# Hedgehog linear attention with a gated feed-forward: the order of work in the load stage, and 28 and 6 unused matmuls in place of 24 and 14

## The chip, the cores and the metric

The kernel runs on one core of one Trainium2 chip. Its time is the device time of one execution in microseconds (us). Before the change three timed runs gave 1631.84 us (median), 1631.5 and 1634.65 us. A further execution, taken by the hardware profiler, took 1630.73 us, of which 1628.6 us lie between its first and its last instruction (its span). All stages below are told in us from the start of that span.

## The reference

Float32 throughout; x has 2048 rows of 576.

```python
def _A_ref(x, wqkv, w_phi, wo):           # linear attention, 32 heads of 18
    q, k, v = split(x @ wqkv)
    pq, pk = q @ w_phi, k @ w_phi         # per head
    phi_q = concat([softmax(pq), softmax(-pq)])
    phi_k = concat([softmax(pk), softmax(-pk)])
    num = phi_q @ (phi_k.T @ v)
    den = phi_q @ sum(phi_k) + 1e-6
    return (num / den) @ wo
def _B_ref(x, w_gate, w_up, w_down):      # 4608 hidden columns
    return (silu(x @ w_gate) * (x @ w_up)) @ w_down
xn = layernorm(x)
return x + _A_ref(xn, ...) * silu(_B_ref(xn, ...))
```

## The kernel before, in words

The program has four stages: load, K and V, Q, and the feed-forward. Only the load stage, the first 69 us, is touched. It brings x and the attention weights into SBUF, normalises x, and turns everything into pairs of a rounded main part (fp32r, "hi", written by a ScalarE cast) and a remainder ("lo", what the cast lost, written by a subtraction on VectorE or GpSimd). Every product of the kernel is then hi·hi + lo·hi + hi·lo.

**x** comes in four blocks of 512 rows, in the order 2, 3, 0, 1; a block is four tiles `xn` of 128 rows. `norm_stats` (lines 173 to 186) makes the statistics on VectorE: two `bn_stats` for each tile, one `bn_aggr`, then six small steps (lines 180 to 186) that end with 1/sqrt in `rs` and the shift in `rt`; the square root in the middle (line 181) is on ScalarE and needs its own activation table. `norm_block` (lines 188 to 219) normalises the four tiles, two on VectorE (line 194) and two on ScalarE (line 191); GpSimd copies the last columns of each tile (line 197); TensorE transposes the tiles into three PSUM buffers `tp`, 24 transposes in all (line 206); ScalarE casts the main parts into `X` (lines 208, 213) and copies the last third to `xr` (line 214); VectorE writes the remainders of the first two thirds (line 209) and GpSimd those of the last (line 216). The function returns the last transpose (`last`), the second remainder on VectorE (`rest`) and the `xr` copy (`copy`).

**The K weights, and later the Q weights,** are multiplied by the feature map at once: `fold` (lines 228 to 238) does five groups of six matmuls of w_qk with the block-diagonal `PHI`, each group into one `tp` buffer, and takes each out with a cast on ScalarE and two subtractions on VectorE (`split_rows`, lines 62 to 65). There are three `tp` buffers for all transposes and folds, so a group starts when the subtractions of the group three before it are through.

**The V weights** come in six pieces `wst` (five buffers, shared with the w_qk pieces). Each is cast on ScalarE into `KVWH` (line 266); four of the remainders are on GpSimd (line 268), two on VectorE (line 270).

**Early tiles.** Two of the 36 hidden column tiles of the feed-forward are computed for blocks 2 and 3 in this stage (lines 116 to 128), which gives TensorE something to do between folds and transposes: for each column tile and each block 14 matmuls for the gate half and 14 for the up half (line 93), a Silu on ScalarE (line 122, another activation table) and a multiplication on VectorE (line 126). Their weights are `raw`, split into `wh` and `wl` by `early_weights` (lines 101 to 114). They use the two PSUM buffers `pe`.

**Unused matmuls** (`keep_clock`, line 141) multiply zeros: 24 at the program's start and 14 behind block 2's transposes. Nothing reads their result.

The order of the instructions on each engine is made by a scheduler from the order in which the code is written, with two means to bend it: `tc.high_priority()` prefers what stands inside it, and `tc.issue_after(i)` puts what stands inside it behind instruction `i`. On the chip each engine takes its own queue strictly in order, and so does the SP engine, which issues the loads.

Of the kernel before, what the change touches and what calls it, by code (L numbers as in the profile page):

```python
# [12 lines left out]
AF = mybir.ActivationFunctionType  # L13
ALU = mybir.AluOpType
# [20 lines left out]
LN_EPS = 1e-5  # L35
# [12 lines left out]
def gated_hedgehog_kernel(ctx: ExitStack, tc, x, w_qk, w_v, w_phi, wo, w_gu, w_tail, w_down, ident_in, mask_in, out):  # L48
# [66 lines left out]

    def early_tile(f, i, parts, js=(0, 1), banks=None, store=nc.sync, behind=None):
        for j in js:
            pg, pu = banks or [eps.tile([P, BT], F32, name="pe") for _ in range(2)]
            xw(pg, i, j, slice(0, BT), *parts[0], False)
            h = epool.tile([P, BT], F32, name="h")  # L120
            with tc.high_priority():
                nc.scalar.activation(h, pg, AF.Silu)
            last = xw(pu, i, j, slice(0, BT), *parts[1], False)
            with tc.issue_after(behind.ins) if behind else ExitStack():
                with tc.high_priority():
                    nc.vector.tensor_mul(h, pu, h)
            store.dma_start(h_dram[i, f, :, j * BT:(j + 1) * BT], h)
        return last

    outs = []  # L130
    with ExitStack() as att:
# [17 lines left out]
        with ExitStack() as wst:  # L149
# [4 lines left out]
            with ExitStack() as pst:  # L154
# [10 lines left out]
                def load_x(b):  # L165
# [5 lines left out]
                    return xns  # L171

                def norm_stats(bs, xns):
                    t = slice(4 * bs[0], 4 * bs[-1] + 4)
# [4 lines left out]
                    var, r, q = mv[:, t, 1], rs[:, t], rt[:, t]  # L179
                    nc.vector.tensor_scalar_add(var, var, LN_EPS)  # L180
                    nc.scalar.activation(r, var, AF.Sqrt)
                    nc.vector.reciprocal(r, r)
                    nc.vector.tensor_mul(q, r, r)
                    nc.vector.scalar_tensor_tensor(q, q, -0.5, var, op0=ALU.mult, op1=ALU.mult)
                    nc.vector.scalar_tensor_tensor(r, q, 1.5, r, op0=ALU.add, op1=ALU.mult)
                    return nc.vector.scalar_tensor_tensor(q, mv[:, t, 0], -1.0, r, op0=ALU.mult, op1=ALU.mult)

                def norm_block(b, xns):
                    for n, (i, xn) in enumerate(zip(range(4 * b, 4 * b + 4), xns)):
                        if n % 2:  # L190
                            nc.scalar.activation(xn[:, 0:D], xn[:, 0:D], AF.Identity, bias=rt[:, i:i + 1],
                                                 scale=rs[:, i:i + 1])
                        else:
                            nc.vector.tensor_scalar(xn[:, 0:D], xn[:, 0:D], mv[:, i, 0:1], rs[:, i:i + 1],
                                                    op0=ALU.subtract, op1=ALU.mult)
# [43 lines left out]

                keep_clock(24)  # L240
                xns = load_x(2)
# [21 lines left out]
                for n in range(6):  # L263
                    k, c = divmod(n, 3)
                    src, vh = wv[n][:, 0:D], KVWH[:, k, c, D:2 * D]
                    nc.scalar.copy(vh, src)
                    if c < 2:
# [8 lines left out]
                for f in range(2):  # L276
                    early_tile(f, 1, first_weights[f], store=nc.gpsimd)

# [850 lines left out]
```

## Time and profile before

| what | value |
|---|---|
| timed runs, median (lowest to highest) | 1631.84 us (1631.5 to 1634.65) |
| profiled execution: own time, span | 1630.73 us, 1628.6 us |
| granted TensorE clock, mean | 0.999 |
| busy over the span: TensorE, VectorE, ScalarE, GpSimd | 99%, 72%, 44%, 40% |
| the chain that ended last | TensorE 94%, VectorE 3%, DMA 1%, ScalarE 1% |
| first matmul of the K and V stage starts at | 69.29 us |

TensorE's share is an average over the program. It is not full in the first 40 us, and the change lies wholly there; so the question is when the load stage lets TensorE go, not what TensorE does later. In a timeline row the columns are start, duration, engine, line and operation, tiles written from tiles read, the count of instructions merged into the row, and in brackets the idle time of the engine before it and what ended it. A row that merges several instructions shows their summed extent.

### The profile page before, as it was taken

How to read it: one execution, taken by the hardware profiler on the slowest of the kernel's cores; microseconds unless marked ns; L12 is line 12 of the kernel's file. 1: busy time of each engine (PE TensorE's matmuls, PEld its weight loads, DVE VectorE, ACT ScalarE, POOL GpSimd, SP SyncE). 2: the span in 40 equal slices, each digit the busy share in tenths (PEclk: the TensorE clock that was granted, in tenths of full speed). 3: DMA queues.
4: the chain of work that ended last, by engine and by line, in shares of the span. 5: the costliest groups of instructions: out<-in, count | busy, mean ns of one | idle time of the engine just before them, and what ended most of it. 6: DMA issues, size and time to landing. Idle time of an engine off the chain costs nothing.

```text
span 1628.6 us, 25267 instructions
## 1 busy us (share of the span) xinstructions
PE 1609.0 (99%) x9422; PEld 1430.2 (88%) x9423; DVE 1172.9 (72%) x1721; ACT 722.1 (44%) x1391; POOL 655.5 (40%) x704
## 2 busy tenths in 40 slices
PE   8999999999999999999999999999999999999998
PEld 5999998999987888888888888888888888888887
DVE  7677769899854678878777778825666766666578
ACT  5633345544433654444454444455433333333334
POOL 4566652434123446446445355313233314133132
PEclk9999999999999999999999999999999999999999
DMA  9522243434247645555454454685454655555444
GB/s 304 190 80 79 93 144 108 127 105 125 62 154 286 214 155 173 171 186 178 167 187 171 161 193 150 249 268 154 140 169 124 203 180 179 168 182 179 141 116 174
DMA packets 121484, 268.46 MB, mean 165 GB/s; under 512 B 12786, under 2 KB 53362, under 8 KB 119570
## 3 DMA queue, kind: packets, MB, share of 16 engines
q1 hardware_dynamic: 106076, 245.44, 45.9%
q0 software_dynamic: 3392, 12.07, 2.6%
q10 hardware_dynamic: 11894, 9.35, 1.8%
q8 instruction: 74, 1.21, 0.3%
q14 instruction: 48, 0.39, 0.1%
HBM read 167.19 MB, written 99.61 MB: 164 GB/s over the span
## 4 chain that ended last, share of the span: by engine, by line
PE 94%; DVE 3%; DMA 1%; ACT 1%; issue 0%; POOL 0%; SPq 0%; ACTq 0%; POOLq 0%; DVEq 0%
PE px L730 24%; PE pd L855 24%; PE pw L730 12%; PE p L93 7%; PE pe L93 7%; PE py L730 6%; PE p L633 4%; PE kvp L312 2%; PE po L613 2%; PE vx L400 1%; PE pt L607 1%; PE vw L400 1%; PE tp L235 1%; PE vy L93 1%; PE vx L93 1%
## 5 line engine op out<-in xcount | busy, mean ns | idle before, releaser
L855 PEld LDWEIGHTS pd<-dw,hh 128*128 128x128 f32 x3048 | 432.5, 188 | 24.2 <-ACT pd L876 1.5
L855 PE MATMUL pd<-dw,hh 128*128 128x288 f32 x3048 | 448.3, 297 | 2.3 <-ACT pd L876 0.7
L730 PE MATMUL px<-X,w 128*128 128x512 f32 x1488 | 384.4, 393 | 2.5 <-ACT s L759 1.4
L730 PEld LDWEIGHTS px<-X,w 128*128 128x128 f32 x1488 | 270.5, 188 | 54.9 <-ACT s L759 3.8
L730 PE MATMUL pw<-X,w 128*128 128x512 f32 x732 | 188.7, 393 | 0.0
L730 PEld LDWEIGHTS pw<-X,w 128*128 128x128 f32 x732 | 137.0, 189 | 30.5
L764 DVE TENSOR_TENSOR s<-pw,s 128x512 f32<-128x512 f32 x124 | 85.1, 688 | 99.6 <-ACT s L759 88.8
L980 DVE TENSOR_TENSOR acc<-pd,acc 128x576 f32<-128x576 f32 x128 | 96.3, 753 | 82.9 <-PE pd L855 82.8
L759 ACT COPY s<-px 128x512 f32<-128x512 f32 x124 | 72.6, 585 | 157.9 <-PE px L730 157.8
L60 DVE TENSOR_TENSOR hh<-ha,hh 128x512 fp32r<-128x512 f32 x140 | 110.9, 818 | 20.7 <-ACT hh L59 19.1
L59 ACT CAST hh<-ha 128x512 fp32r<-128x512 f32 x140 | 82.6, 619 | 92.3 <-PE pd L855 73.6
L93 PE MATMUL pe<-X,wh 128*128 128x512 f32 (+1 forms) x380 | 119.6, 398 | 2.2 <-DVE X L209 1.0
L952 POOL TENSOR_TENSOR hb<-hb 128x512 f32<-128x512 f32 x34 | 46.5, 1368 | 165.7 <-DVE hb L776 161.3
L60 DVE TENSOR_TENSOR w<-ld,w 128x512 fp32r<-128x512 f32 (+1 forms) x93 | 77.2, 831 | 35.8 <-ACT w L59 34.7
L730 PE MATMUL px<-X,wt 96*128 96x512 f32 x248 | 97.9, 395 | 0.0
L730 PE MATMUL py<-X,w 128*128 128x512 f32 x372 | 96.4, 393 | 0.0
L965 POOL TENSOR_TENSOR ha<-ha 128x512 f32<-128x512 f32 x34 | 52.6, 1562 | 106.2 <-DVE hh L60 106.2
L939 POOL TENSOR_TENSOR h<-ha,hb 128x512 f32<-128x512 f32 x34 | 44.3, 1303 | 123.9 <-DVE ha L780 88.6
L59 ACT CAST w<-ld 128x512 fp32r<-128x512 f32 (+1 forms) x93 | 51.0, 549 | 89.6 <-POOL ld L720 58.0
L93 PEld LDWEIGHTS pe<-X,wh 128*128 128x128 f32 (+1 forms) x380 | 69.8, 189 | 16.1 <-DVE X L209 1.4
L784 ACT COPY py<-px 128x512 f32<-128x512 f32 x62 | 35.5, 572 | 102.6 <-PE px L730 85.0
L717 POOL TENSOR_TENSOR ts<-ld 128x256 f32<-128x256 f32 x31 | 28.7, 926 | 125.7 <-issue 68.5
(267 smaller groups left out, 3251.9 us busy)
## 6 DMA issues: line engine op xcount, KB each, us to landing
w_dram<-w SPq DMA_DIRECT2D x90, 512.0 KB
w<-w_dram SPq DMA_DIRECT2D x90, 512.0 KB
wt<-t_dram SPq DMA_DIRECT2D x61, 336.0 KB
ld<-in_B_w_gu SPq DMA_DIRECT2D x31, 512.0 KB
X<-sum_dram SPq DMA_DIRECT2D x8, 1280.0 KB
rt<-in_B_w_down SPq DMA_DIRECT2D x33, 288.0 KB
rb<-in_B_w_down SPq DMA_DIRECT2D x33, 288.0 KB
w_dram<-w SPq DMA_DIRECT2D x30, 256.0 KB
```

Of the source, the lines that this page charges most:

```text
L59: nc.scalar.copy(hi, src)
L60: nc.vector.tensor_sub(lo, src, hi)
L93: last = nc.tensor.matmul(ps, l, r, start=n == 0, stop=n == len(pairs) - 1)
L633: nc.tensor.matmul(ps[:, 0:HALF], a[0:w, g, jc], bw[0:w, g, n], start=k == 0, stop=k == 3 * NG - 1)
L730: nc.tensor.matmul(ps, l, r, start=first and n == 0, stop=last and n == len(mm) - 1, skip_group_check=True)
L759: nc.scalar.copy(t, ps)
L764: nc.vector.tensor_add(t, ps, t)
L855: nc.tensor.matmul(ps, l, r, start=first and n == 0 and m == 0, stop=n == len(hs) - 1 and m == 2, skip_group_check=True)
L939: sub(s, g["h"][0][0], g["h"][0][1])
L952: nc.gpsimd.tensor_add(a21, a21, g["h"][1][1])
L965: sub(a12, a12, g["h"][0][0])
L980: nc.vector.tensor_add(a2, pd[:, :, 0:HALF], a2)
```

## The change

Five edits, all in the load stage:

1. The first run of unused matmuls has 28 instead of 24, the second 6 instead of 14.
2. The statistics of block 3 are put behind the second VectorE remainder of block 2 (`rest`), where they stood behind the last small step of block 2's statistics; the small steps are at high priority.
3. The second early column tile's weights (`early_weights(1)`) are put behind block 3's `xr` copy.
4. The six casts of the V weights are put behind the same copy.
5. The Silu of the first early column tile for each block is held behind the second ScalarE normalisation of block 3.

```diff
-    def early_tile(f, i, parts, js=(0, 1), banks=None, store=nc.sync, behind=None):
+    def early_tile(f, i, parts, js=(0, 1), banks=None, store=nc.sync, hold=None, behind=None):
...
-            with tc.high_priority():
-                nc.scalar.activation(h, pg, AF.Silu)
+            with tc.issue_after(hold.ins) if hold else ExitStack():
+                with tc.high_priority():
+                    nc.scalar.activation(h, pg, AF.Silu)
...
+                    with tc.high_priority():
+                        nc.vector.tensor_scalar_add(var, var, LN_EPS)
+                        roots.append(nc.scalar.activation(r, var, AF.Sqrt))
...
-                keep_clock(24)
+                keep_clock(28)
...
-                chain = norm_stats([2], xns[0:4])
+                norm_stats([2], xns[0:4])
                 last, rest, _ = norm_block(2, xns[0:4])
                 with tc.issue_after(last.ins):
-                    keep_clock(14)
+                    keep_clock(6)
+                with tc.issue_after(rest.ins):
+                    norm_stats([3], xns[4:8])
                 first_weights = [early_weights(0)]
-                with tc.issue_after(chain.ins):
-                    norm_stats([3], xns[4:8])
                 fold(wk, KVWH[:, :, :, 0:D], KVWL[:, :, :, 0:D])
-                norm_block(3, xns[4:8])
-                first_weights.append(early_weights(1))
+                _, _, copy = norm_block(3, xns[4:8])
+                first_weights.append(early_weights(1, copy))
...
-                    nc.scalar.copy(vh, src)
+                    with tc.issue_after(copy.ins):
+                        nc.scalar.copy(vh, src)
...
-                    early_tile(f, 1, first_weights[f], store=nc.gpsimd)
+                    early_tile(f, 1, first_weights[f], store=nc.gpsimd, hold=None if f else norms[3])
```

What this makes of the queues is seen at three places. Line numbers of the changed kernel are one to five higher than those of before from line 122 on.

VectorE, at block 2's remainders (X_64 and X_65 are its two X buffers). Before:

```order
L194 TENSOR_SCALAR xn<-xn,mv,rs 128x576 x2
L177 BN_STATS stats<-xn 128x6
L209 TENSOR_TENSOR X_64<-tp,X_64 128x1024
L209 TENSOR_TENSOR X_65<-tp,X_65 128x1024
L177 BN_STATS stats<-xn 128x6 x2
```

Now:

```order
L198 TENSOR_SCALAR xn<-xn,mv,rs 128x576 x2
L213 TENSOR_TENSOR X_64<-tp,X_64 128x1024
L213 TENSOR_TENSOR X_65<-tp,X_65 128x1024
L180 BN_STATS stats<-xn 128x6 x3
L181 BN_AGGR mv<-stats 128x2
```

One `bn_stats` of block 3 has moved from ahead of the two remainders to behind them.

VectorE, from the second step before the end of block 3's statistics to block 3's normalisation, while the K fold is taken out (KVWL, KVWH). Before:

```order
L185 SCALAR_TENSOR_TENSOR rs<-rt,rs 128x4
L177 BN_STATS stats<-xn 128x6
L186 SCALAR_TENSOR_TENSOR rt<-mv,rs 128x4
L64 TENSOR_TENSOR KVWL<-tp,KVWH 128x4x126
L64 TENSOR_TENSOR wl<-raw,wh 128x512
L65 TENSOR_TENSOR wh<-raw,wh 32x2x128
L65 TENSOR_TENSOR KVWH<-tp,KVWH 32x2x126
L64 TENSOR_TENSOR KVWL<-tp,KVWH 128x4x72
L65 TENSOR_TENSOR KVWH<-tp,KVWH 32x2x72
L194 TENSOR_SCALAR xn<-xn,mv,rs 128x576 x2
```

Now:

```order
L189 SCALAR_TENSOR_TENSOR rs<-rt,rs 128x4
L65 TENSOR_TENSOR KVWH<-tp,KVWH 32x2x126
L190 SCALAR_TENSOR_TENSOR rt<-mv,rs 128x4
L64 TENSOR_TENSOR KVWL<-tp,KVWH 128x4x126
L65 TENSOR_TENSOR KVWH<-tp,KVWH 32x2x126
L64 TENSOR_TENSOR KVWL<-tp,KVWH 128x4x72
L65 TENSOR_TENSOR KVWH<-tp,KVWH 32x2x72
L198 TENSOR_SCALAR xn<-xn,mv,rs 128x576 x2
```

A `bn_stats` of block 0 and the two subtractions of the second early weights (wl, wh) are gone from ahead of the normalisation; they stand behind it now.

ScalarE, from block 3's square root to its X casts. Before:

```order
L266 CAST KVWH<-wst 128x576
L181 ACTIVATE rs<-mv 128x4
L266 CAST KVWH<-wst 128x576
L63 CAST KVWH<-tp 128x6x126
L63 CAST wh<-raw 128x768
L63 CAST KVWH<-tp 128x6x72
L191 ACTIVATE xn<-xn,rt,rs 128x576 x2
L122 ACT_TABLE_LOAD
L122 ACTIVATE h<-pe 128x512
L266 CAST KVWH<-wst 128x576 x2
L208 CAST X_66<-tp 128x1024
```

Now:

```order
L185 ACTIVATE rs<-mv 128x4
L63 CAST KVWH<-tp 128x6x126
L63 CAST KVWH<-tp 128x6x72
L195 ACTIVATE xn<-xn,rt,rs 128x576 x2
L123 ACT_TABLE_LOAD
L123 ACTIVATE h<-pe 128x512
L212 CAST X_66<-tp 128x1024
```

The V weights' casts (from `wst`) and the second early weights' cast (from `raw`) are gone from this stretch. Behind block 3's `xr` copy there now stand, in this order, a `wh` cast, the two x_dram stores, one V cast, a Silu, the other `wh` cast, four V casts, and behind the square root and a Silu of the next pair of blocks the sixth V cast, ahead of that pair's ScalarE normalisations. On TensorE 13 matmuls of the first early column tile now stand between the third and the fourth group of the K fold, where six stood. On SP the sixth V piece and all five w_qk pieces for Q stand behind the loads of x blocks 0 and 1 and behind the second a_dram store; before, all six V pieces and one w_qk piece stood ahead of the last four x tiles.

More of the change, by code (lines that the diff above doesn't have):

```diff
@@ L171, in load_x @@
                     return xns
+                roots, norms = [], []
                 def norm_stats(bs, xns):
@@ L179, in norm_stats @@
                     var, r, q = mv[:, t, 1], rs[:, t], rt[:, t]
[L180 to L186, printed above, removed]
+                    with tc.high_priority():
+                        nc.vector.tensor_scalar_add(var, var, LN_EPS)
+                        roots.append(nc.scalar.activation(r, var, AF.Sqrt))
+                        nc.vector.reciprocal(r, r)
+                        nc.vector.tensor_mul(q, r, r)
+                        nc.vector.scalar_tensor_tensor(q, q, -0.5, var, op0=ALU.mult, op1=ALU.mult)
+                        nc.vector.scalar_tensor_tensor(r, q, 1.5, r, op0=ALU.add, op1=ALU.mult)
+                        nc.vector.scalar_tensor_tensor(q, mv[:, t, 0], -1.0, r, op0=ALU.mult, op1=ALU.mult)
                 def norm_block(b, xns):
@@ L190, in norm_block @@
                         if n % 2:
-                            nc.scalar.activation(xn[:, 0:D], xn[:, 0:D], AF.Identity, bias=rt[:, i:i + 1],
-                                                 scale=rs[:, i:i + 1])
+                            norms.append(nc.scalar.activation(xn[:, 0:D], xn[:, 0:D], AF.Identity,
+                                                              bias=rt[:, i:i + 1], scale=rs[:, i:i + 1]))
                         else:
```

## The prediction

> **What bounds the kernel now.** First the stages: for a stretch in us, what each engine was busy, then the granted clock, the share of the DMA engines, GB/s.
>
> ```profile
> core 0: us, PE busy (x) PEld busy (x) DVE busy (x) ACT busy (x) POOL busy (x), PEclk, DMA share, GB/s
> 31.80:39.00 7.20, 5.66 (x36) 4.50 (x36) 7.11 (x14) 6.09 (x9) 4.49 (x7) 1.00 0.96 337
> 39.00:50.10 11.10, 11.10 (x47) 8.92 (x48) 10.27 (x30) 5.89 (x8) 4.71 (x8) 1.00 0.99 366
> 50.10:69.30 19.20, 19.20 (x141) 17.73 (x140) 10.57 (x15) 13.64 (x19) 7.08 (x18) 1.00 0.52 178
> ```
>
> From 39.0 us on TensorE is full (11.10 of 11.10, then 19.20 of 19.20), at clock 1.00. Ahead of that it is not, and VectorE is: 7.11 of 7.2 us, and still 10.27 of 11.1 afterwards. So the load stage's end is TensorE's remaining work counted from the last place where it waited, and VectorE's queue decides when that is. Its waits up to 70 us (in total, times, longest):
>
> ```profile
> PE tp L206 <- DVE xn L194: 1.9, 1, 1.9
> PE tp L235 <- ACT KVWH L266: 1.0, 1, 1.0
> PE pe L93 <- DVE X L209: 1.0, 1, 1.0
> PE tp L206 <- ACT h L122: 0.9, 1, 0.9
> PE pe L93 <- DVE h L126: 0.5, 1, 0.5
> ```
>
> The first is block 2's transposes, which need normalised x and stay where they are. The other four, 3.4 us, lie between 23 and 39 us. With the second run of unused matmuls they are what there is to win. In two of them the view names ScalarE, but VectorE's subtraction or normalisation ended in the 0.15 us before, as the rows below show. Behind 39 us comes one dense stretch up to the first matmul of the next stage, which is itself dense at once:
>
> ```profile
> 69.29 0.30 PE L93 MATMUL p<-KVWH,X 128*128 128x288 f32 x1
> ```
>
> A gain is thus a gain at 69.29 us, and it is handed on. I found no wait later in the program on a clock of its own.
>
> **The change, step by step. One: the fold's start.**
>
> ```profile
> 1.32 7.87 PE L141 MATMUL pe<-idle 128*128 128x512 bf16 x24 [1.32 <-POOL idle L136]
> 13.53 1.93 ACT L208 CAST X<-tp 128x1024 fp32r<-128x1024 f32 x2 [1.37 <-PE tp L206]
> 14.42 3.19 PE L141 MATMUL pe<-idle 128*128 128x512 bf16 x13
> 15.24 0.46 DVE L177 BATCH_NORM_STATS2 stats<-xn 128x6 f32<-128x288 f32 x1 [3.77 <-DMA xn<-in_A_x]
> 15.61 2.34 DVE L209 TENSOR_TENSOR X<-tp,X 128x1024 fp32r<-128x1024 f32 x2
> 17.44 4.18 PE L235 MATMUL tp<-PHI,wst 126*128 126x126 f32 x36
> ```
>
> The four unused matmuls more at the start lie inside the first wait: the run ends at 9.19 and block 2's transposes start at 11.0, so 4 x 0.22 us go into a 1.9 us wait and cost nothing. If that cover were gone they would cost 0.9. The second run, listed as 13, takes 3.19 us or 0.23 apiece (by 14), and the K fold stands right behind it at 17.44. With six it ends at 14.42 + 6 x 0.23 = 15.8. The fold also needs a `tp` buffer, which the first remainder (L209) frees. Now that remainder is queued behind a `bn_stats` which waited 3.77 us for its x tile until 15.24. With the statistics behind it, it starts when the first cast is done, 13.53 + 0.97 = 14.5, and ends 1.17 later, at 15.7. The fold starts at 15.8, 1.6 earlier. That alone is no gain yet: the fourth group waits for VectorE.
>
> **Two: VectorE up to block 3's normalisation.**
>
> ```profile
> 23.54 0.42 DVE L65 TENSOR_TENSOR KVWH<-tp,KVWH 32x252 fp32r<-32x252 f32 x1
> 24.06 2.87 PE L235 MATMUL tp<-PHI,wst 126*128 126x126 f32 x24 [1.04 <-ACT KVWH L266]
> 24.18 2.85 POOL L268 TENSOR_TENSOR KVWL<-wst,KVWH 128x576 fp32r<-128x576 f32 x2 [4.19 <-ACT rs L181]
> 9.93 0.16 DVE L184 SCALAR_TENSOR_TENSOR rt<-rt,mv 128x4 f32<-128x4 f32 x1
> 26.24 0.81 DVE L184 SCALAR_TENSOR_TENSOR rt<-rt,mv 128x4 f32<-128x4 f32 x1
> 27.61 0.45 DVE L177 BATCH_NORM_STATS2 stats<-xn 128x6 f32<-128x288 f32 x1
> 28.76 0.68 DVE L64 TENSOR_TENSOR wl<-raw,wh 128x512 fp32r<-128x512 f32 x1
> 29.45 0.42 DVE L65 TENSOR_TENSOR wh<-raw,wh 32x256 fp32r<-32x256 f32 x1
> 31.11 1.07 DVE L194 TENSOR_SCALAR xn<-xn,mv,rs 128x576 f32<-128x576 f32 x2
> 31.83 2.81 PE L206 MATMUL tp<-ident,xn 128*128 128x128 f32 x24 [0.87 <-ACT h L122]
> ```
>
> VectorE's queue starts 1.1 us earlier (15.61 to 14.5) and has one `bn_stats` of about 0.4 more behind the remainders: 0.7 earlier at the subtraction that lets the fourth group go (23.54, and the group at 24.06 right behind it becomes 23.4). TensorE's wait there is filled by the 13 early matmuls that now stand ahead of it. From 23.54 to the normalisation at 31.11 the queue took 7.57 us. Out of that go the second early weights (0.68 + 0.42), block 0's `bn_stats` (0.45), and a stretch: a step over 4 columns took 0.81 here and 0.16 in block 2, beside GpSimd's V remainders, which move away. That is 1.10 + 0.45 + 0.65 = 2.2. The normalisation starts at 31.11 - 0.7 - 2.2 = 28.2, and with it the transposes, 31.83 to 28.9: **2.9 us earlier**. TensorE has 11 early matmuls to do between the fold and there, 2.6 us at the 0.237 that the 47 in 39.00:50.10 take, so it is only just there before the data, and the former 0.9 us wait all but goes.
>
> **Three: to the last wait.**
>
> ```profile
> 28.16 1.63 ACT L191 ACTIVATE xn<-xn,rt,rs 128x576 f32<-128x576 f32 x2 [0.55 <-DVE rt L186]
> 29.81 1.28 ACT L122 ACT_TABLE_LOAD   x1
> 31.11 0.60 ACT L122 ACTIVATE h<-pe 128x512 f32<-128x512 f32 x1
> 33.15 1.93 ACT L208 CAST X<-tp 128x1024 fp32r<-128x1024 f32 x2 [0.32 <-PE tp L206]
> 35.92 1.06 ACT L214 COPY xr<-tp 128x1024 f32<-128x1024 f32 x1
> 37.12 2.51 POOL L216 TENSOR_TENSOR X<-xr,X 32x512 fp32r<-32x512 f32 x2 [2.71 <-ACT xr L214]
> ```
>
> Two waits (1.0 and 0.5) were left behind the transposes. In their place I expect one. ScalarE's normalisations start when VectorE's statistics end, 1.7 us ahead of VectorE's own normalisation as the new queue stands (four subtractions between), so at 26.9 once the fold's last cast is out. Then 1.63 + 1.28 + 0.60 bring the Silu to 30.4, where the hold changes nothing: the table load comes behind the normalisations in both kernels. X casts at 30.4 (their transposes are then there), the `xr` copy 2.77 after them as before, its end at 34.3, GpSimd's first remainder 0.14 + 1.25 later at 35.7. TensorE has 14 early matmuls (3.3 us) behind transposes that end near 31.6, so it comes there at 34.9 and waits 0.9 where it waited 1.5. It has also done one early matmul more ahead of the transposes. Sum so far: 2.9 + 0.6 + 0.2 = 3.7; less 0.3 for a Q fold group that comes out short of a buffer, since the dense stretch now has fewer early matmuls between its groups: **3.4**.
>
> **Four: what is given back.** The remaining danger is block 0, whose transposes are next.
>
> ```profile
> 33.00 1.41 POOL L268 TENSOR_TENSOR KVWL<-wst,KVWH 128x576 fp32r<-128x576 f32 x1
> 33.37 1.66 DVE L270 TENSOR_TENSOR KVWH<-wst,KVWH 32x576 fp32r<-32x576 f32 x1
> 39.70 1.43 POOL L268 TENSOR_TENSOR KVWL<-wst,KVWH 128x576 fp32r<-128x576 f32 x1
> 40.69 1.06 DVE L270 TENSOR_TENSOR KVWH<-wst,KVWH 32x576 fp32r<-32x576 f32 x1
> 47.95 2.04 DVE L194 TENSOR_SCALAR xn<-xn,mv,rs 128x576 f32<-128x576 f32 x4
> 50.11 0.49 PE L206 MATMUL tp<-ident,xn 128*128 128x128 f32 x3
> ```
>
> These are the two V remainders on VectorE (L270), each beside one on GpSimd. The first met GpSimd at 33.37 with 1.04 left of its operation and took 1.66; the second at 40.69 with 0.44 left and took 1.06. The difference of 0.60 is that of what GpSimd had left: VectorE stood still until GpSimd was through, and did some 0.62 of its own. Both its operands are in SBUF; the L64 and L126 steps, which read PSUM, and `bn_stats`, with one operand, show nothing of the kind. The Trainium skill says it in SBUF — State Buffer, section "SBUF: two separate sides": the two engines share a port pair under "an exclusive lock", which a VectorE operation with two SBUF inputs takes against a reading GpSimd operation, and the loser blocks for the whole of it. The trace agrees, with those 0.60 us; by the rule the change would keep what is worked out next, without it the 3.4.
>
> VectorE took 47.95 - 31.11 = 16.84 us from block 3's to block 0's normalisation. To that come the second early weights (1.10) and a `bn_stats` (0.45); the V remainder that moves behind goes (1.06), and the block of the other (0.60). With no new blocks block 0's normalisation stands at 28.2 + 16.84 + 1.55 - 1.66 = 44.9 and the first tile is ready at 45.5, ahead of TensorE, which comes there 3.4 us earlier than 50.11, at 46.7. But GpSimd now does its two X remainders and all four V remainders from 34.5 to about 45, just where VectorE has five steps with two SBUF inputs (four subtractions of early weights, one V remainder). A block cost 1.04 and 0.44 in the rows, 0.74 in the mean. None blocked is one end; five blocked, 3.7, the other. I take three, since two run right behind their like: 2.2. Then the tile is ready at 47.7 and TensorE waits **1.0**. At five it waits 2.5.
>
> The other moved waits cost nothing by themselves. Behind the V casts on ScalarE stand a square root and its table load, which wait for VectorE anyway (46.6 us before). On SP the w_qk pieces for Q are queued behind GpSimd's V remainders and the second a_dram store, so some of them leave later than now.
>
> ```profile
> 41.16 0.91 SPq L225 DMA_DIRECT2D wst<-in_A_w_qk  x2
> 18.97 4.38 DMA wst<-in_A_w_v
> ```
>
> Today the last leave from 41.2 us on and are read only behind block 0's transposes; a V piece took 4.4 us to land. With issues from 41 to 45 they are there by 50 to 52, about when the fold asks. If that cover were gone each us of lateness is a us.
>
> **The sum.** 3.4 - 1.0 = 2.4 us off the profiled execution: 1630.73 becomes 1628.3. The median of the runs is 1.1 above that execution, so on its scale 1631.84 - 2.4 = **1629.4 us**, or 0.15% less. A measurement of this kernel tells about 0.2% (3.3 us) from no change, so most of this forecast lies within "same".
>
> **The rivals.** (a) *VectorE is not blocked*, or GpSimd yields. For it: GpSimd's copies at 29 us did not lengthen the 0.42 us subtraction at 29.45. Against: the 0.60. The gain is 3.4, or 3.7 with all buffers free; if GpSimd's remainders come sooner too, the 0.9 us wait goes and it is 4.6: 1628.4 to 1627.2. (b) *VectorE is blocked each time*, and block 0's normalisation takes over as the bound: 3.4 - 2.5 = 0.9, 1630.9; if every load were late to match, nothing, and the change only moves the wait from block 3 to block 0. (c) *Slower: the sixth V piece.* Its cast stands on ScalarE ahead of block 0's normalisations, and its load stands on SP behind GpSimd's first V remainder (38 us) and 1280 KB of a_dram store. Issued at 38.4 it should land near 43 at 4.4 us; ScalarE is there at 46 to 48. From a landing at 48 on, each us later is a us for ScalarE, the transposes and the end, and past 48 + 2.4 = 50.4 the change is a loss; 0.2% slower is reached at a landing near 54, 15 us behind its issue, or 1635.1 and more, 1638 at 57. For it speaks a DMA share of 0.96 to 0.99 from 31.8 to 50.1 us; against it, that loads ahead of it leave earlier too.
>
> **How the numbers follow.** The forecast (2.4, from 1.2 to 3.3) gets 0.46; (a) 0.36, nearly all of it over the 0.2% line, which lies at 1628.6; (b) 0.06; (c) 0.12. So faster 0.36, same 0.46 + 0.06 = 0.52, slower 0.12. The range goes from 1626.9, below (a)'s best, to 1633.0, a little into (c).
>
> **What would show it.** In the changed kernel's profile: the K fold near 15.8 us instead of 17.44; block 3's transposes near 28.9 instead of 31.83; a wait of about 0.9 us on GpSimd's remainder near 35 us; L64 and L65 of the second early weights, or the V remainder, longer than 0.68, 0.42 and 0.62 beside GpSimd between 35 and 45 us; a wait of about 1 us at block 0's first transpose, near 47; the first matmul of the next stage near 66.9 instead of 69.29. The prediction is wrong if block 3's transposes do not move (then VectorE's queue was not the bound), if no wait follows at block 0 (rival a), or if the wait there names a `wst` load or ScalarE's V cast (rival c).

## The result, and the profile after

| | before | changed |
|---|---|---|
| timed runs, median (lowest to highest) | 1631.58 us (1630.55 to 1634.65, 21 runs) | 1629.62 us (1628.36 to 1632.42, 21 runs) |
| ratio to before, 95% interval | | 0.9987 [0.9981, 0.9993] |
| profiled execution, span | 1628.6 us | 1628.1 us |
| first matmul of the next stage | 69.29 us | 67.86 us |

The change is faster by 0.13%, 2.1 us with an interval of 1.1 to 3.1, and under the 0.2% from which the prediction counts a difference. The forecast was 1629.4 us. A second set of 11 runs of the changed kernel gave 1628.96 us against 1632.11, ratio 0.9986 [0.9977, 0.9995]. Inside the profile the forecast did less well: it had the first matmul of the next stage at 66.9 us, 2.4 earlier, and it came 1.43 earlier; in a second profile of the changed kernel it came at 68.50, 0.79 earlier. So the question is where the rest went. That the runs gained more than the profiles show is no riddle of its own: 1.43 lies within the interval, and the one profiled execution of the kernel before (1630.73 us) was 0.85 faster than the median of its runs, while the two of the changed kernel (1629.89 and 1629.91) were 0.3 and 0.95 slower than theirs.

Two of the stretches shown before, in the changed kernel (columns as in the prediction: busy times of TensorE, its weight loads, VectorE, ScalarE and GpSimd, then granted clock, DMA share, GB/s):

```profile
31.80:39.00 7.20, 6.39 (x29) 4.63 (x28) 7.14 (x11) 4.60 (x8) 4.92 (x4) 1.00 0.96 325
39.00:50.10 11.10, 9.30 (x40) 6.85 (x39) 10.49 (x25) 7.10 (x11) 6.63 (x8) 1.00 0.94 307
```

Up to 39 us TensorE is fuller than it was (6.39 us for 5.66). Behind 39 us, where it was full, it now loses 1.8 us of 11.1. Its waits from 9 to 75 us, but for one of 0.2, say where (total, times, longest):

```profile
PE tp L210 <- DVE xn L198: 0.8, 1, 0.8
PE pe L93 <- DVE h L127: 0.8, 1, 0.8
PE pe L93 <- POOL X L220: 0.8, 1, 0.8
PE pe L93 <- ACT wh L63: 0.5, 1, 0.5
```

The timeline shows block 2's transposes, the fold's start, block 3's transposes, the last wait ahead of 39 us, the two waits that stand in place of a dense stretch, and the first matmul of the next stage:

```profile
10.55 0.44 PE L210 MATMUL tp<-ident,xn 128*128 128x128 f32 x2
15.36 4.28 PE L239 MATMUL tp<-PHI,wst 126*128 126x126 f32 x36
29.11 2.81 PE L210 MATMUL tp<-ident,xn 128*128 128x128 f32 x24
36.03 0.73 PE L93 MATMUL pe<-X,wh 96*128 96x512 f32 x2 [0.81 <-POOL X L220]
44.64 0.47 PE L93 MATMUL pe<-X,wh 128*128 128x512 f32 x1 [0.82 <-DVE h L127]
49.00 0.87 PE L210 MATMUL tp<-ident,xn 128*128 128x128 f32 x3 [0.84 <-DVE xn L198]
67.86 0.30 PE L93 MATMUL p<-KVWH,X 128*128 128x288 f32 x1
```

The fold stood at 17.44, block 3's transposes at 31.83. The fourth row waits for GpSimd's remainder, as forecast. At 44.64 a half of an early tile wants its PSUM buffer back from the multiplication L127, and at 49.00 the transposes of block 0 want normalised x. Both are on VectorE, and this is its queue there, with GpSimd's beside it:

```profile
35.11 1.42 DVE L64 TENSOR_TENSOR wl<-raw,wh 128x512 fp32r<-128x512 f32 x1
36.56 1.40 DVE L65 TENSOR_TENSOR wh<-raw,wh 32x256 fp32r<-32x256 f32 x1
40.31 1.90 DVE L64 TENSOR_TENSOR wl<-raw,wh 128x512 fp32r<-128x512 f32 x1
42.24 1.53 DVE L65 TENSOR_TENSOR wh<-raw,wh 32x256 fp32r<-32x256 f32 x1
43.81 0.69 DVE L127 TENSOR_TENSOR h<-pe,h 128x512 f32<-128x512 f32 x1
48.28 1.55 DVE L198 TENSOR_SCALAR xn<-xn,mv,rs 128x576 f32<-128x576 f32 x3
34.72 2.96 POOL L220 TENSOR_TENSOR X<-xr,X 32x512 fp32r<-32x512 f32 x2
37.75 1.49 POOL L273 TENSOR_TENSOR KVWL<-wst,KVWH 128x576 fp32r<-128x576 f32 x1
40.23 3.27 POOL L273 TENSOR_TENSOR KVWL<-wst,KVWH 128x576 fp32r<-128x576 f32 x2 [0.99 <-ACT KVWH L271]
```

The four subtractions of the second early weights took 0.68 and 0.42 us in the kernel before; here 1.42, 1.40, 1.90 and 1.53, so **4.05 us more** (6.25 less 2 x 1.10). Each of them lies over a GpSimd subtraction. The multiplication at 43.81 stands right behind the last, and block 0's normalisation 4.5 us further on.

Not all that is earlier in this profile is the change's doing. Block 2's transposes, which the change leaves alone, start at 10.55 us and started at 11.04 before, because the x tiles landed earlier in this execution; in all profiles of kernels with 28 unused matmuls they start anywhere from 10.4 to 11.9 us. In the second profile of the changed kernel they start as before. The row of the kernel before, then those of the second profile:

```profile
11.04 0.44 PE L206 MATMUL tp<-ident,xn 128*128 128x128 f32 x2 [1.85 <-DVE xn L194]
```

```profile
10.99 0.44 PE L210 MATMUL tp<-ident,xn 128*128 128x128 f32 x2 [1.40 <-DVE xn L198]
23.57 0.42 DVE L65 TENSOR_TENSOR KVWH<-tp,KVWH 32x252 fp32r<-32x252 f32 x1
29.73 2.81 PE L210 MATMUL tp<-ident,xn 128*128 128x128 f32 x24
68.50 0.30 PE L93 MATMUL p<-KVWH,X 128*128 128x288 f32 x1
```

So about 0.5 us of the 1.43 is this execution's luck, and block 3's transposes came 2.1 us earlier by the like comparison, not 2.7.

### The profile page after: what moved, and what is told of

It is laid out like the page before. It is cut to its first block, busy times and chain, and to the rows that moved or that the text cites. A ratio compares the mean times of both kernels' runs of the same rounds, so it can differ in the third digit from the quotient of the medians.

```text
span 1628.1 us, 25265 instructions
## 1 busy us (share of the span) xinstructions
PE 1609.4 (99%) x9418; PEld 1429.7 (88%) x9419; DVE 1172.2 (72%) x1721; ACT 722.6 (44%) x1391; POOL 659.0 (40%) x704
## 4 chain that ended last, share of the span: by engine, by line
PE 94%; DVE 3%; DMA 2%; issue 0%; ACT 0%; POOL 0%; SPq 0%; ACTq 0%; POOLq 0%; DVEq 0%
PE px L735 24%; PE pd L860 24%; PE pw L735 12%; PE p L93 7%; PE pe L93 6%; PE py L735 6%; PE p L638 4%; PE kvp L317 2%; PE po L618 2%; PE vx L405 1%; PE pt L612 1%; PE vw L405 1%; PE vy L93 1%; PE vx L93 1%; DMA wst<-in_A_w_qk 0%
## 5 line engine op out<-in xcount | busy, mean ns | idle before, releaser
L60 DVE TENSOR_TENSOR hh<-ha,hh 128x512 fp32r<-128x512 f32 x140 | 112.4, 828 | 20.7 <-ACT hh L59 19.1
L60 DVE TENSOR_TENSOR w<-ld,w 128x512 fp32r<-128x512 f32 (+1 forms) x93 | 77.2, 832 | 35.9 <-ACT w L59 34.9
```

The lines of the kernel that those rows point to most:

```text
L60: nc.vector.tensor_sub(lo, src, hi)
```

## Experiments

**Theory 1**, from the prediction: VectorE stands still while a GpSimd operation holds a lock that both need, and the give-back is that time. **Theory 2**: the give-back comes from the casts that were moved on ScalarE, or from loads that come later, and L64 and L65 are long for the same reason or for none that matters. Beside them stands the question which of the five edits brings the gain.

**One: the same queues with a shorter GpSimd operation.**

```diff
-                        nc.gpsimd.tensor_sub(KVWL[:, k, c, D:2 * D], src, vh)
+                        nc.gpsimd.tensor_copy(KVWL[:, k, c, D:2 * D], vh)
```

> The changed kernel, but GpSimd copies the main part of the V weights into the remainder's tile (one input) instead of subtracting (two inputs), four times; so the remainders of V are left out of the result. The order on every engine is unchanged. Theory 1, VectorE stands still while a GpSimd operation with two SBUF inputs runs: the second pair of L64 and L65 of the second early weights goes from 1.90 and 1.53 us to about 0.68 and 0.42, the first pair, which meets the X remainders, stays at about 1.4 each; block 0's normalisation starts 2.3 us earlier, near 46; both waits of TensorE behind 43 us (0.82 and 0.84) go; the first matmul of the next stage moves from 67.86 to about 66.2, the time falls by 1.4 to 1.7 us. Theory 2, the give-back comes from the moved casts on ScalarE or from late loads: L64 and L65 may change, but the two waits and 67.86 stay within 0.3.

Measured: 1628.9 us, ratio 0.9982 [0.9973, 0.999]. The timeline of this kernel, VectorE, GpSimd, then TensorE:

```profile
40.11 1.11 DVE L64 TENSOR_TENSOR wl<-raw,wh 128x512 fp32r<-128x512 f32 x1
41.26 0.85 DVE L65 TENSOR_TENSOR wh<-raw,wh 32x256 fp32r<-32x256 f32 x1
40.02 0.67 POOL L273 CAST KVWL<-KVWH 128x576 fp32r<-128x576 f32 x1 [1.73 <-ACT KVWH L271]
66.20 0.30 PE L93 MATMUL p<-KVWH,X 128*128 128x288 f32 x1
```

The first matmul of the next stage is at 66.20, where theory 1 put it; the order on every engine, with its casts and loads, is that of the changed kernel (only the `wst` buffers come free a little sooner, and nobody waits for them), so theory 2 falls. Block 0's normalisation came at 46.61. The wait for L127 is gone; of that at block 0 0.44 us stayed, since TensorE came earlier too. One detail was wrong: the two subtractions did not go back to 0.68 and 0.42. They were still held by 0.43 each, and GpSimd's copies last 0.67 us: a copy with one input holds VectorE as well, only for less long. The runs alone would not have shown it: the ratio of 0.9982 lies within the interval of the changed kernel's 0.9987, so the 1.4 to 1.7 us are shown by the trace and not by the times.

**Two: the lock by itself.** A small kernel runs pairs of operations on tiles of their own.

> A small kernel by itself, which computes nothing of the reference: VectorE runs one kind of operation three or four times, first alone, then beside a run of GpSimd operations on other tiles (128x576 subtractions; then copies, 128x128 copies with a repeated input, memsets). Theory 1, one lock for both engines, which a VectorE operation with two SBUF inputs needs and a reading GpSimd operation holds: the VectorE subtraction of two SBUF tiles takes 0.7 us alone and up to 1.4 more beside GpSimd subtractions, less beside copies, nothing more beside memsets; subtraction from PSUM, bn_stats, tensor_scalar, copy stay within 0.1 us of their time alone; the 128x4 step with two SBUF inputs goes from 0.16 to up to 1.4. Theory 2, plain sharing of bandwidth: all VectorE operations that read SBUF become longer by a like share (10 to 50%), and none by a whole GpSimd operation.

Rows of VectorE (three or four operations each), and below them some of what GpSimd did meanwhile (its subtractions are L60, copies L63, small copies with a repeated input L66, memsets L70):

```profile
34.50 2.14 DVE L45 TENSOR_TENSOR vr<-ps,va 128x512 f32<-128x512 f32 x3 [0.79 <-ACT va L82]
37.75 1.95 DVE L48 BATCH_NORM_STATS2 st<-va 128x6 f32<-128x288 f32 x4 [1.11 <-ACT va L82]
53.23 2.14 DVE L42 TENSOR_TENSOR vr<-va,vs 128x512 f32<-128x512 f32 x3 [0.79 <-ACT va L82]
56.17 4.62 DVE L42 TENSOR_TENSOR vr<-va,vs 128x512 f32<-128x512 f32 x3 [0.79 <-ACT va L82]
61.58 2.83 DVE L42 TENSOR_TENSOR vr<-va,vs 128x512 f32<-128x512 f32 x3 [0.79 <-ACT va L82]
16.17 4.32 DVE L51 TENSOR_SCALAR vr<-va,vs 128x576 f32<-128x576 f32 x3 [2.76 <-ACT va L82]
21.48 4.32 DVE L54 COPY vr<-va 128x576 f32<-128x576 f32 x3 [0.99 <-ACT va L82]
26.80 2.37 DVE L57 SCALAR_TENSOR_TENSOR vr<-va,vs 128x4 f32<-128x4 f32 x3 [1.00 <-ACT va L82]
47.70 1.45 DVE L54 COPY vr<-va 128x576 f32<-128x576 f32 x3 [2.56 <-ACT va L82]
51.69 0.76 DVE L57 SCALAR_TENSOR_TENSOR vr<-va,vs 128x4 f32<-128x4 f32 x4 [2.54 <-ACT va L82]
37.23 4.35 POOL L60 TENSOR_TENSOR gr<-ga,gs 128x576 f32<-128x576 f32 x3 [0.78 <-ACT ga L79]
47.16 3.22 POOL L66 COPY gr<-ga 128x128 f32<-128x128 f32 x8 [0.77 <-ACT ga L79]
51.14 3.09 POOL L70 MEMSET gr<- 128x568 f32 x5 [0.76 <-ACT ga L79]
55.02 5.22 POOL L60 TENSOR_TENSOR gr<-ga,gs 128x576 f32<-128x576 f32 x3 [0.79 <-ACT ga L79]
61.01 2.86 POOL L63 COPY gr<-ga 128x576 f32<-128x576 f32 x3 [0.77 <-ACT ga L79]
```

With an operand in PSUM (L45) or as `bn_stats` (L48), VectorE runs at 0.71 and 0.49 us apiece beside GpSimd's subtractions. A subtraction of two SBUF tiles (L42) takes 0.71 beside memsets, which here cover the first half of the row (alone it took 0.72), 0.94 beside copies and 1.54 beside subtractions. The step over four columns (L57) takes 0.19 beside memsets and 0.79 in the mean beside subtractions. That is theory 1; shared bandwidth would have slowed `bn_stats` too. The expectation failed on L51 and L54: `tensor_scalar` and a copy, with one SBUF input, take 1.44 beside subtractions (the shortest of them took 0.58 and 0.46), as the two-input operation does. GpSimd's small copies with a repeated input, of the kind that `norm_block` makes, are an exception: beside them VectorE's copy takes 0.48, about its shortest, while they themselves go from 0.30 to as much as 0.44. That agrees with what rival (a) of the prediction had pointed at, the copies at 29 us. And GpSimd loses as well: three subtractions take 4.35 us beside `bn_stats` and 5.22 beside L42, 0.29 more apiece.

**Three: no VectorE subtraction to hold up.** The second early weights' four subtractions go to GpSimd.

```diff
-    def split_rows(hi, lo, src):
+    def split_rows(hi, lo, src, eng=nc.vector):
...
-        nc.vector.tensor_sub(lo, src[:, :, 0:2], hi[:, :, 0:2])
+        eng.tensor_sub(lo, src[:, :, 0:2], hi[:, :, 0:2])
...
-                    split_rows(hi, lo, raw)
+                    split_rows(hi, lo, raw, nc.gpsimd if f == 1 else nc.vector)
```

> The changed kernel, with the four subtractions of the second early weights on GpSimd instead of VectorE (the same values). Nothing is left out. Theory 1: VectorE loses 6.25 us ahead of block 0 (1.42, 1.40, 1.90, 1.53), of which 4.05 were blocking; its V remainder (L275) may be blocked once (0.7 to 1.4 more). The second early weights are first read at 44.6 us, GpSimd has them by 42.5. Both waits of TensorE behind 43 us go; what may be left is a wait for GpSimd's copies of x, which now stand behind a V remainder that ends near 47. First matmul of the next stage 66.2 to 66.8 instead of 67.86, the time 1.1 to 1.7 us less. Rival: GpSimd becomes the bound, its V remainders, and with them the w_qk loads and the copies, come 2 to 4 us late, first matmul 68 or later.

Measured: 1632.87 us, ratio 1.0006 [0.9997, 1.0015]. The whole gain is gone, and the first matmul of the next stage stands at 72.92 instead of the expected 66.2 to 66.8. VectorE in this kernel, from the reciprocal of block 0's statistics on, and GpSimd beside it:

```profile
45.25 0.98 DVE L187 TENSOR_TENSOR rt<-rs 128x8 f32<-128x8 f32 x1
46.26 1.34 DVE L188 SCALAR_TENSOR_TENSOR rt<-rt,mv 128x8 f32<-128x8 f32 x1
47.64 1.91 DVE L189 SCALAR_TENSOR_TENSOR rs<-rt,rs 128x8 f32<-128x8 f32 x1
44.78 2.79 POOL L273 TENSOR_TENSOR KVWL<-wst,KVWH 128x576 fp32r<-128x576 f32 x2
```

I had counted GpSimd's queue and overlooked what it now stands beside: three steps over eight columns, 0.17 us each in the changed kernel, were held for 3.72 us in all, and block 0's normalisation, which needs them, came at 49.67. TensorE waited 3.4 us. What follows costs as much again; two stretches of this kernel (busy times, granted clock):

```profile
12.00:14.70 2.70, 2.66 (x14) 2.65 (x14) 0.00 (x0) 0.53 (x1) 1.66 (x7) 0.50 1.02 272
50.30:55.40 5.10, 5.01 (x16) 3.96 (x17) 2.85 (x5) 2.63 (x4) 4.65 (x13) 0.50 0.97 305
```

Behind two waits of TensorE (2.2 us to 11.4, 3.4 us to 50.4) the granted clock is 0.50, for about 3.4 and 5.5 us; at half the clock that is 1.7 and 2.7 us of work lost. The experiment tells against this cure, and it shows theory 1 once more, but its time is not the price of the lock alone.

**Four: which edit brings the gain.** Edit 1 alone, then the changed kernel with one edit undone (edit 4 also in part).

Edit 1 alone (28 and 6 in the kernel before):

> The kernel before with 28 and 6 unused matmuls and nothing else. Theory: the K fold starts near 16.8 instead of 17.44 (the first remainder of block 2 still stands behind a late bn_stats and frees the buffer at 16.8 at the earliest), but block 3 waits for VectorE's queue as before, and the scheduler now puts a Silu with its table load ahead of ScalarE's normalisations of block 3 (1.9 us): block 3's transposes at 31.8 or up to 1.9 later, first matmul of the next stage 69.3 to 71, the time 0 to 1.7 us above the kernel before. Rival, the unused matmuls are what costs: first matmul 67.5 to 68, the whole gain.

Measured: 1632.37 us, ratio 1.0003 [0.9995, 1.0012]; the fold at 16.91, block 3's transposes from 32.15, the first matmul of the next stage at 70.50. As the theory had it: the unused matmuls go, and VectorE and ScalarE are no sooner ready.

Edit 1 undone (24 and 14 in the changed kernel):

> The changed kernel with 24 and 14 unused matmuls (edit 1 undone). Theory 1: the K fold starts near 17.3, block 3's transposes a little later than 29.08, but VectorE's queue up to block 0's normalisation, with the blocking by GpSimd in it, is what bounds; TensorE's waits of 0.8, 0.8 and 0.8 take in the 1.85 us of eight matmuls: first matmul of the next stage 67.8 to 68.4, the time within 0.5 us of the changed kernel's. Rival, the unused matmuls count in full: 69.7, 1.8 us more.

Measured: 1631.55 us, ratio 0.9997 [0.9988, 1.0006], where the changed kernel on the same chip had 1628.96. The expectation failed: the other four edits without this one are worth nothing either. A stretch of its profile:

```profile
11.40:18.80 7.40, 6.94 (x30) 5.63 (x31) 3.30 (x5) 4.91 (x7) 2.23 (x8) 0.55 0.99 322
```

The 24 matmuls were through at 8.2, TensorE waited 3.65 us for block 2, and the clock stood near half until about 18; the fold started at 20.71. How much of the 2.6 us is this clock, how much the eight matmuls and how much the order that the scheduler made of it, one profile does not tell.

Edit 2 undone:

```diff
-                norm_stats([2], xns[0:4])
+                chain = norm_stats([2], xns[0:4])
...
-                with tc.issue_after(rest.ins):
+                with tc.issue_after(chain.ins):
                     norm_stats([3], xns[4:8])
```

> The changed kernel, with block 3's statistics behind the last small step of block 2's again (edit 2 undone, the small steps still at high priority). A bn_stats that waits for its x tile until about 15.2 us stands ahead of block 2's first remainder again, so the K fold starts near 16.8 instead of 15.36, and VectorE's queue is up to 1.4 us later at the fold's fourth group. Theory: block 3's transposes start near 30 instead of 29.08 (one of VectorE's two normalisations now stands ahead of the fold's last subtractions, so the first tile is ready at once), and since block 0's normalisation bounds, the first matmul of the next stage moves by what VectorE's queue is late, 0 to 1.4: 67.9 to 69.3. Rival, edit 2 brings nothing beyond the fold's start: 67.9.

Measured: 1631.52 us, ratio 0.9996 [0.9987, 1.0005]: the gain is gone. The fold started at 18.12 and the first matmul stands at 71.83. In this profile too the clock was low, 0.51 from 12.8 to 16.0 us, which is some 1.6 us of work, and block 2's transposes started at 11.29, 0.7 later than in the changed kernel's first profile. With both taken off, which is an estimate, the first matmul is at 69.5, near the upper end of what the theory allowed and far from the rival's 67.9.

Edit 3 undone (`early_weights(1)` without `copy`):

> The changed kernel without edit 3: the first pair of subtractions of the second early weights stands ahead of block 3's normalisation, where no GpSimd subtraction runs. Theory 1: that pair takes 0.68 and 0.42 there instead of 1.42 and 1.40, so block 3's transposes come 1.1 to 1.4 us later, near 30.3, and block 0's normalisation about 0.6 to 1.7 earlier than 48.28, near 47; the waits behind 43 us shrink by what TensorE comes later; first matmul of the next stage 67.0 to 67.9: edit 3 is worth nothing or less. Theory 2, no blocking by GpSimd and the load is what counts: the 1.2 us at block 3 come through, first matmul near 69.

Measured: 1631.65 us, ratio 1.0004 [0.9995, 1.0013]; the first matmul at 69.36, above the expected 67.0 to 67.9. VectorE's rows in this kernel:

```profile
37.34 0.46 DVE L180 BATCH_NORM_STATS2 stats<-xn 128x6 f32<-128x288 f32 x1 [1.13 <-DMA xn<-in_A_x]
42.88 3.05 DVE L275 TENSOR_TENSOR KVWH<-wst,KVWH 32x576 fp32r<-32x576 f32 x2
```

The first pair is unheld, as said (0.69 at 26.93). But the queue, no longer filled by it at 35 us, came to a `bn_stats` whose x tile had not landed and waited 1.13 us, and both V remainders (L275) now stood in the stretch and were held for 1.55 (3.05 less 2 x 0.75). Block 0's normalisation came at 48.15 instead of 48.28: what was saved was spent on the next two things in the queue. TensorE waited 1.31 us there and then ran at a clock of 0.54 from 51.0 to 54.6, some 1.7 us of work; without that the first matmul would be near 67.7, where theory 1 had it. By the times edit 3 is needed; in this profile the reason is the stretch at half clock, which neither theory had. That it comes in most executions is likely but not shown: nine of the eleven have a mean clock below 0.999, of the changed kernel's 12 of 32.

Edit 4 undone, twice:

```diff
-                    with tc.issue_after(copy.ins):
-                        nc.scalar.copy(vh, src)
+                    nc.scalar.copy(vh, src)
```

> The changed kernel without edit 4: the V casts stand where the scheduler puts them, three of them between the casts of the K fold, so three V remainders run on GpSimd before 34 us. Theory 1: the second pair of L64 and L65 meets GpSimd once at most, so 1.2 to 2.3 us of blocking go; against it stand small steps of block 3's statistics beside GpSimd (0.65) and one V remainder more on VectorE ahead of block 3's normalisation (0.6 to 1.7): transposes of block 3 near 30.3 instead of 29.08, waits of TensorE behind 43 us gone, first matmul of the next stage 67.0 to 67.9, the time within 0.9 of the changed kernel's. Theory 2, edit 4 is what brought the gain of 29.08: transposes near 31.5 and first matmul near 69.

> The changed kernel without edit 4, once more. Theory 1: first matmul of the next stage at 67.0 to 67.3, 0.75 earlier than the changed kernel's, and the time 0.5 to 1.0 us less than the changed kernel's on the same chip. Rival, the two do not differ, and the first comparison was that of two chips: within 0.3.

> The changed kernel itself, beside the next three on one chip. Theory 1: first matmul of the next stage at 67.7 to 68.0 as in its first profile, waits of 0.8 and 0.8 behind 43 us; the time 1.3 to 2.0 us less than the kernel before. If a wait of over 1 us is followed by a stretch at half the granted clock, 1.7 to 1.9 us more.

Measured: 1628.71 us, ratio 0.9984 [0.9976, 0.9993]; in the second set 1628.87, 0.9982 [0.9973, 0.9991], beside 1628.96 for the changed kernel. First matmul at 67.11, 0.75 earlier than 67.86, in the first profile:

```profile
30.52 2.81 PE L210 MATMUL tp<-ident,xn 128*128 128x128 f32 x24 [1.50 <-DVE xn L198]
42.15 0.68 DVE L64 TENSOR_TENSOR wl<-raw,wh 128x512 fp32r<-128x512 f32 x1
```

The second pair is unheld (0.68, 0.42) since three V remainders are through by then, block 3's transposes are 1.4 us later, and there is no wait behind 39 us: the lock's time is back, and paid for at block 3. In the second pair of profiles the first matmuls were at 70.03, behind 3.8 us at a clock of 0.55, and at 68.50 for the changed kernel, whose block 2 was transposed 0.4 later than in its first profile and which had the same two waits (0.8 and 0.9). So the times decide: the two kernels do not differ by what these runs can tell, and edit 4 brings nothing that they show.

Edit 4 for VectorE's two casts only:

```diff
-                    with tc.issue_after(copy.ins):
+                    with tc.issue_after(copy.ins) if c == 2 else ExitStack():
```

> The changed kernel with edit 4 kept only for the two casts whose remainders are on VectorE; the other four stand where the scheduler puts them. Theory 1: VectorE has neither a V remainder ahead of block 3's normalisation (0.75 in v_casts_back) nor GpSimd's V remainders beside the second pair of early weights; block 3's transposes near 30.1, first matmul of the next stage 66.5 to 67.3, the time 0.6 to 1.4 us less than the changed kernel's. Rival, the new order of VectorE's small steps (a multiplication of an early tile now stands among them) takes it back: 67.5 to 68.

Measured: 1631.44 us, ratio 0.9995 [0.9986, 1.0004], and the first matmul at 70.05; the expectation failed. TensorE waited 2.5 us up to 35.8 for a remainder on VectorE; that stood behind a `bn_stats` which waited for its x tile, and started at 34.54:

```profile
32.57 0.82 DVE L180 BATCH_NORM_STATS2 stats<-xn 128x6 f32<-128x288 f32 x2 [1.26 <-DMA xn<-in_A_x]
```

With the V remainder out of the queue VectorE reached the statistics of block 0 before the tile was there. The multiplication at 49.66 is the rival's: it stands among block 0's small steps and waited 0.81 for TensorE.

Edit 5 undone:

> The changed kernel without edit 5. The scheduler then puts the first Silu with its table load between the two ScalarE normalisations of block 3, so the second of them comes 1.9 us later. Theory: 9 of the 24 transposes start near 29, the rest near 30.7; the X casts, the copy and GpSimd's remainders come 1.5 to 1.9 later, so the wait at 36 us ends near 37.5; behind it VectorE's queue is as long as before, and block 0's normalisation, which bounds, moves by 0 to 1: first matmul of the next stage 67.9 to 69. Rival, the hold does nothing (as the prediction had it): 67.9 and all else the same.

Measured: 1630.05 us, ratio 0.9991 [0.9983, 1.0]; nine transposes from 28.60 and fifteen from 30.26, the first matmul at 68.26, 0.4 later. That is in the lower part of the expected range, and at block 3 the mechanism is the theory's. Behind it it is not: the wait at 36 us ended at 36.3 and not at 37.5, and block 0's normalisation came at 47.46, 0.8 earlier than in the changed kernel and not later. TensorE's waits there are 1.47 us for that normalisation and 0.53 for GpSimd's copies, where the changed kernel has 0.82 and 0.84, so the range was met for another reason. The time lies between those of the two kernels, and these runs cannot tell it from the changed kernel's.

## Why the prediction was right or wrong, point by point

- **The fold's start.** Forecast 15.8, measured 15.36, in the second profile 15.82, there with block 2's transposes where they stood before. Right. That it is no gain by itself was right too (edit 1 alone). But "cost nothing" for the four unused matmuls at the start counted only their time. The same 28 took 7.7 to 9.2 us in these profiles, and the wait between them and block 2 was anything from none to 2.5 us. Where that wait is long the clock falls behind it, and four matmuls more shorten it.
- **VectorE up to block 3.** From the subtraction that lets the fourth group go to the normalisation the queue was to take 2.2 us less than 7.57; it took 5.44 in both profiles, 2.1 less, by the three parts that were named. Right. That this subtraction comes 0.7 earlier was not. It came at 22.95 in the first profile, 0.6 earlier, of which 0.5 is block 2's earlier start, and at 23.57 in the second, no earlier than before (23.54). The fold had become earlier than the first early weights: ScalarE waited 1.88 us for their load, VectorE for ScalarE's cast of them, and TensorE 0.51 us at 20.6:

```profile
18.74 0.83 ACT L63 CAST wh<-raw 128x768 fp32r<-128x768 f32 x1 [1.88 <-DMA raw<-in_B_w_gu]
20.60 0.69 DVE L64 TENSOR_TENSOR wl<-raw,wh 128x512 fp32r<-128x512 f32 x1 [0.31 <-ACT wh L63]
```

  So the transposes came 2.1 us earlier by the like comparison, and not 2.9. That the first profile has them at 29.11, near the forecast 28.9, is in part luck.
- **To the last wait.** Forecast a wait of 0.9 us that ends at 35.8; measured 0.81, to 36.03. Right. That "the hold changes nothing" was not: without edit 5 the scheduler puts the table load between ScalarE's two normalisations, for 0.4 us in the profiles. The 0.3 us for a Q fold group short of a buffer did not come: none of TensorE's waits up to 75 us is at the Q fold.
- **What is given back: the step that failed, by its size.** "I take three, since two run right behind their like: 2.2." It was four, and 4.05 us. The mean of 0.74 came from two meetings in which GpSimd had 1.04 and 0.44 left. Here GpSimd's operations follow each other with hardly a gap, so a VectorE step that gets through meets the next one nearly whole: 0.74, 0.98, 1.22 and 1.11 us. The V remainder, the fifth candidate, was free (0.75 at 44.53). Two things stood against these 1.85 us more. The sum had an error the other way: of the V remainder that stays it took out 0.60, the difference of the two blocks, where by its own rows 1.04 was the block. And by the starts of their rows `bn_stats` and the aggregations took 0.26 us less than before, where 0.45 more had been added. So VectorE took 19.89 us from block 3's to block 0's normalisation where 18.9 had been worked out, and came to block 0 at 48.28 instead of 47.1. Only one wait was foreseen; the multiplication L127 behind the last held step gave a second one, and the two make 1.66 us instead of 1.0.
- **The moved casts and loads** cost nothing, as said: none of TensorE's waits names a `wst` tile, and the sixth V piece's cast stands at 49.13, for 0.66 us, and TensorE had no wait for ScalarE's normalisations behind it. Rival (c) is out, and so is (a).
- **The sum.** 2.4 us were forecast at the first matmul; the first profile shows 1.43, the second 0.79. Of the 3.4 ahead of the give-back, 3.1 and 2.5 came (1.43 + 1.66 and 0.79 + 1.69); of the 1.0 given back it was 1.7 in both. That the median moved by 1.96 us and met the forecast within 0.2 is therefore not to its credit: at the first matmul the sum was 1.0 to 1.6 us too large. The times are too coarse to tell; their interval, 1.1 to 3.1, holds the forecast and the first profile's figure alike. The mean clock of an execution does not settle it either. It is 0.999 in 20 of 32 executions of the changed kernel that are listed with one and in 19 of 92 of the kernel before, but it also falls with an idle end: in the first profile of the changed kernel the clock is 1.00 in the whole load stage and 0.50 from 1622 us on, where TensorE has no work left. That the 28 matmuls make a stretch at half clock in the load stage rarer fits the profiles, and was not tried by itself.

## What to carry to other kernels

When work is moved behind a point, look at what the other engine runs there at that time: a VectorE step with two inputs in SBUF, or a copy or `tensor_scalar` from SBUF to SBUF, queues with GpSimd's subtractions instead of running beside them, and a chain of 0.17 us steps cost 1.2 us more apiece here. When GpSimd's operations stand back to back, count most of one for each such step (0.7 to 1.2 us of 1.25 to 1.5 here), not a mean of what happened to be left. When a step is brought forward, look at which load it now waits for. Compare times in two profiles only from a point that the change leaves alone: block 2 alone moved by 0.5 us between two executions. And undo edits one at a time before crediting any: without edit 1, 2 or 3 the times cannot be told from those of the kernel before, so none of the three carries the gain alone, and for edit 4 the runs show none.

## What the runs showed of the hardware

- A reading GpSimd operation of 128x576 holds up VectorE whether it has one input or two (0.43 us behind a 0.67 us copy); memsets do not, nor did copies of 128x128 with a repeated input (VectorE's copy 0.48 beside them). VectorE's `tensor_scalar` and copy from SBUF to SBUF are held beside subtractions as two-input operations are (1.44 us for about 0.5). The prediction had quoted from the Trainium skill, SBUF — State Buffer, section "SBUF: two separate sides", only the case of two inputs; the rule there also names VectorE's two-port modes, which fits these two rows.
- TensorE's granted clock can fall to half after short waits, and need not after longer ones. It fell after 2.2, 2.5, 3.4 and 3.65 us, but also after 1.6 us in one profile and 1.31 in another, each time for about 3.4 us or twice that (6.8 and 6.9); after twelve others of 1.3 to 1.9 us and one of 2.51 us (edit 4 for two casts, at 35.8) it did not. At the program's end it fell 1.1 to 4.2 us after the last matmul in six profiles. The Trainium skill, TensorE: Matmul & The Clock Gate, section "Part 1: The HAM clock gate (the "warmup" mystery)", has a free-running window of about 3.4 us in which an idle TensorE loses the full clock. The 3.4 us agree, and so does the chance in it; but no wait of a whole window was needed here, one of less than half of it was enough.
